# Linformer attention and a gated feed-forward in one kernel: all turns of batch 1 by DMA, later loads for batch 2, wider weight slices and one slice issued earlier

## Chip, cores and metric

One core of one Trainium2 chip runs the kernel. The metric is device time in microseconds, the median over runs.

## The reference, cut

```python
k_proj = einsum('ks,bhsd->bhkd', E, k); v_proj = einsum('ks,bhsd->bhkd', F, v)   # 8 batches, 8 heads, 1024 x 64
scores = q @ k_proj^T / 8                 # 64 projected keys
attn   = softmax(scores); x = attn @ v_proj               # then [8192, 512]
out    = (silu(x @ w_gate) * (x @ w_val)) @ w_out         # d_ff 1536; float32 out
```

## The kernel before

Batches are numbered from 0, so "the second batch" is batch 1. Attention is split into two halves (`ch`) a batch and four units a half. Half a batch is also one chunk of 512 tokens of the feed-forward part, which goes through 12 features of 128 columns: a gate product, a value product, and a third of an output product of the previous chunk. Attention of the next batch is laid into slots between those products: slot 2t follows the gate product of step t, slot 2t+1 the value and output ones.

q must be turned before the scores, and the normalised scores must be turned before the product with v. Both turns exist in two forms:

```python
BY_DMA = [(b, ch) for b in range(1, B) for ch in range(CH)][1:]     # all halves from (1, 1) on

def u_T(b, u, at="a", eng=nc.scalar):        # q, on TensorE: four transposes and a copy from PSUM
    ...
    for n in range(4):
        nc.tensor.transpose(out=ps[:, n, :], in_=src[...], identity=ident_bf[:])
    copy(eng, t[:], ps[:])

def u_TD(b, ch):                             # q, half a batch at once, by DMA from SyncE
    t = aw.tile([P, 2 * H, P], BF16, name="qTd", tag="qTd")
    nc.sync.dma_start_transpose(out=t[:], in_=qb[b, ch][:].rearrange("p h j d -> p (h j d)"))

def u_A(b, u, eng=nc.vector): ...            # normalised scores, on TensorE: four transposes and a copy
def u_AD(b, ch): ...                         # the same, half a batch at once, by DMA from SyncE
```

GpSimd issues every load of q, k, v and the weights (float32 in HBM, bf16 in SBUF), in program order and between its normalisations `u_N`. As built, each load also waits for the landing of the eighth load before it. In the start:

```python
u_N(0, 0)
load_w_gv(1, 2, (1,))
...                                      # (cut) u_N(0, 2), u_N(0, 1): GpSimd waits for scores here
load_w_gv(2, 4)                          # gate and value weights of features 2 and 3: 256 columns
...                                      # (cut)
load_w_gv(4, 6)
load_q(0, 1)
for f in (6, 8, 10):
    load_w_gv(f, f + 2)
load_wo(0); load_wo(1); load_k(1)
```

The softmax here doesn't subtract the row's maximum and nothing guards it: scores larger than these inputs give would overflow.

## Time and profile before

| | before |
|---|---|
| time, median of its runs beside the changed kernel | 573.17 us (573.05 to 573.64) |
| span of the profile | 571.7 us |
| TensorE matmuls | 2971, busy 99% of the span |
| DMA transposes | 13 of q, 13 of normalised scores |
| TensorE holes after the first feed-forward product that wait for weights | 0.60 us (feature 6, gate) and 0.28 us (feature 6, value) |

The page and the timeline lines of before stand in the prediction. A timeline line gives start, length, engine, source line, operation, out<-in, shapes and count, and in brackets the idle time before it and what ended it. Its start times matter more than the lengths: a 512-column matmul is shown as 0.38 us, but the next one starts 0.216 us after it. A hole is a start-to-start distance beyond that.

### The profile page before, as it was taken

To read this page: it belongs to the slowest core of one execution; us is meant where nothing else is said; L and a number is where in the kernel's file an instruction comes from. 1 tells how busy PE (TensorE), PEld (TensorE's weight loads), DVE (VectorE), ACT (ScalarE), POOL (GpSimd) and SP (SyncE) were. 2 spreads that over 40 slices of the span, in tenths; PEclk is the share of its full clock that TensorE was granted. 3 is DMA by queue.
4 is the path that set the end of the run, shared out by engine and by line. 5 is a ranking of instruction groups with operands and counts; after the bars stand their busy time and mean duration, and the time that the engine had idled before them with its cause. 6 is when DMAs were issued, how large, how long until landed. Compare 5 with 4: busy or idle time off the path is not lost.

```text
span 571.7 us, 7944 instructions
## 1 busy us (share of the span) xinstructions
PE 564.2 (99%) x2971; PEld 268.5 (47%) x2971; DVE 336.6 (59%) x581; ACT 238.3 (42%) x421; POOL 109.2 (19%) x122
## 2 busy tenths in 40 slices
PE   8999999999999999999999999999999999999997
PEld 4644444444444444444444444444444444444444
DVE  3677566666466654666556665567546674554540
ACT  3555434354435434444335434354342543443232
POOL 6834121134002500124001330023200220000000
PEclk9999999999999999999999999999999999999999
DMA  9999993549901697038940499204990124100012
GB/s 202 176 199 206 202 177 77 89 71 197 202 29 47 113 192 148 19 75 129 196 100 37 64 176 196 63 20 90 196 176 37 44 50 75 38 37 23 33 38 92
DMA packets 106983, 61.86 MB, mean 108 GB/s; under 512 B 60096, under 2 KB 98240, under 8 KB 106944
## 3 DMA queue, kind: packets, MB, share of 16 engines
q0 software_dynamic: 42800, 29.36, 35.7%
q1 hardware_dynamic: 63232, 30.42, 24.7%
q10 hardware_dynamic: 912, 1.57, 1.0%
q8 instruction: 23, 0.38, 0.3%
q14 instruction: 16, 0.13, 0.1%
HBM read 60.29 MB, written 16.78 MB: 135 GB/s over the span
## 4 chain that ended last, share of the span: by engine, by line
PE 92%; DMA 3%; DVE 2%; POOL 1%; ACT 1%; issue 0%; DVEq 0%; POOLq 0%
PE yps L362 29%; PE vps L324 27%; PE gps L324 27%; PE kvp L149 3%; PE sc L229 2%; PE pv L287 2%; DMA wv<-in_moe_w_val_dram 2%; DMA qb<-in_q_dram 1%; DVE zz L244 1%; POOL AA L260 0%; POOL wg L117 0%; PE qTp L195 0%; DVE hT L348 0%; ACT xT L137 0%; DVE s L343 0%
## 5 line engine op out<-in xcount | busy, mean ns | idle before, releaser
L343 DVE SCALAR_TENSOR_TENSOR s<-th,gps 128x512 f32<-128x512 f32 x192 | 130.5, 680 | 139.2 <-ACT th L336 138.8
L324 PE MATMUL gps<-xT,wg 128*128 128x512 bf16 (+1 forms) x776 | 197.8, 377 | 0.7 <-DMA wg<-in_moe_w_gate_dram 0.4
L324 PE MATMUL vps<-xT,wv 128*128 128x512 bf16 (+1 forms) x776 | 197.5, 377 | 0.1
L362 PE MATMUL yps<-wo,hT 128*128 128x512 bf16 (+1 forms) x780 | 194.5, 376 | 0.0
L336 ACT ACTIVATE th<-gps 128x512 f32<-128x512 f32 x192 | 114.6, 597 | 163.4 <-PE gps L324 161.9
L348 DVE TENSOR_TENSOR hT<-s,vps 128x512 bf16<-128x512 f32 x192 | 132.0, 687 | 22.1 <-PE vps L324 1.5
L362 PEld LDWEIGHTS <-hT 128*128 128x128 bf16 x780 | 76.2, 98 | 89.9
L260 POOL TENSOR_TENSOR AAd<-ee,rr 128x512 bf16<-128x512 f32 x52 | 54.1, 1040 | 319.5 <-issue 178.1
L324 PEld LDWEIGHTS <-wv 128*128 128x128 bf16 x776 | 73.8, 98 | 83.2 <-issue 3.3
L324 PEld LDWEIGHTS <-wg 128*128 128x128 bf16 x776 | 74.0, 98 | 81.9 <-DMA wg<-in_moe_w_gate_dram 0.9
L372 ACT ACTIVATE ysb<-yps 128x512 f32<-128x512 f32 (+1 forms) x65 | 38.4, 590 | 78.1 <-PE yps L362 78.1
L137 ACT CAST xT<-pv 128x512 bf16<-128x512 f32 x63 | 36.7, 584 | 51.2 <-PE pv L287 50.3
L244 DVE TENSOR_REDUCE zz<-ee 128x8 f32<-128x512 f32 x64 | 43.5, 679 | 19.4 <-ACT ee L233 19.4
L233 ACT ACTIVATE ee<-sc 128x512 f32<-128x512 f32 x64 | 37.9, 596 | 18.0 <-PE sc L229 17.9
L287 PE MATMUL pv<-AT,BDV 128*128 128x512 bf16 x60 | 22.6, 379 | 0.0
L229 PEld LDWEIGHTS <-qTd 128*128 128x128 bf16 x208 | 16.0, 98 | 12.3
L229 PE MATMUL sc<-BD,qTd 128*128 128x128 bf16 x208 | 20.1, 219 | 0.0
L137 DVE CAST BDV<-kvp 64x256 bf16<-64x256 f32 x14 | 6.0, 427 | 22.1 <-ACT ks L159 19.1
L260 POOL TENSOR_TENSOR AA<-ee,rr 128x512 bf16<-128x512 f32 x11 | 11.4, 1038 | 36.3 <-DVE rr L246 34.4
L246 DVE RECIPROCAL rr<-zz 128x8 f32<-128x8 f32 x64 | 13.0, 203 | 6.7 <-DVE zz L244 0.5
L149 PE MATMUL kvp<-vb,FT 128*64 128x512 bf16 (+2 forms) x80 | 15.7, 339 | 0.3 <-ACT BDV L137 0.3
L149 PE MATMUL kvp<-kb,ET 128*64 128x512 bf16 (+1 forms) x72 | 15.5, 358 | 0.3 <-DVE kb L137 0.2
(51 smaller groups left out, 146.4 us busy)
## 6 DMA issues: line engine op xcount, KB each, us to landing
out_dram<-ysb SPq DMA_DIRECT2D x63, 256.0 KB, 2.4
qb<-in_q_dram POOLq DMA_DIRECT2D x15, 512.0 KB, 16.9
kb<-in_k_dram POOLq DMA_DIRECT2D x7, 1024.0 KB, 11.3
vb<-in_v_dram POOLq DMA_DIRECT2D x7, 1024.0 KB, 14.0
wo<-in_moe_w_out_dram POOLq DMA_DIRECT2D x2, 768.0 KB, 15.3
wg<-in_moe_w_gate_dram POOLq DMA_DIRECT2D x5, 256.0 KB, 9.6
wv<-in_moe_w_val_dram POOLq DMA_DIRECT2D x5, 256.0 KB, 10.2
kraw<-in_k_dram ACTq DMA_DIRECT2D x2, 512.0 KB, 5.0
```

The costliest lines, as they stand in the source:

```text
L137: (nc.scalar.copy if eng is nc.scalar else eng.tensor_copy)(out=out, in_=in_)
L149: nc.tensor.matmul(out=t[lo : lo + 64, h0:h1].rearrange("p h d -> p (h d)"), lhsT=w[:, j, :], rhs=src[b][:, h0:h1, j, :], start=(j == 0), ...
L229: nc.tensor.matmul(out=ps[:, n, :], lhsT=t[:, n, :], rhs=BD[b % 2][:, 4 * g + n, :], start=True, stop=True)
L233: nc.scalar.activation(out=e[:].rearrange("p h j k -> p (h j k)"), in_=ps[:].rearrange("p a k -> p (a k)"), func=AF.Exp, scale=scale,)
L244: nc.vector.reduce_sum(out=z[:], in_=e[:], axis=AX.X)
L260: eng.tensor_tensor(out=a.rearrange("p j h k -> p h j k"), in0=ee.pop((b, u))[:], in1=rr.pop((b, u))[:].unsqueeze(3).to_broadcast([P, 4, 2 ...
L324: nc.tensor.matmul(out=ps[:, ts], lhsT=(wg, wv)[w][:, kt, f * P : (f + 1) * P], rhs=x[:, kt, ts], start=(kt == 0), stop=(kt == NKT - 1),)
L336: nc.scalar.activation(out=th[:], in_=ps[:], func=AF.Tanh, scale=0.5)
L343: nc.vector.scalar_tensor_tensor(out=s1[:], in0=th[:], scalar=1.0, in1=g[:], op0=ALU.add, op1=ALU.mult)
L348: nc.vector.tensor_tensor(out=hT[c][:, f, :], in0=s1[:], in1=ps[:], op=ALU.mult)
L362: nc.tensor.matmul(out=yy[c][:, cs], lhsT=hT[c][:, f, i * P : (i + 1) * P], rhs=wo[:, f, cs], start=(f == 0), stop=(f == NFT - 1),)
L372: nc.scalar.activation(out=ysb[:, cs], in_=yy[c][:, cs], func=AF.Copy, scale=0.5)
```

## The change

Its intent: take the last TensorE turns outside batch 0 off the busiest engine, place the loads so that the DMA turns come in time, and load weights in fewer and larger transfers. Core of the diff:

```diff
-BY_DMA = [(b, ch) for b in range(1, B) for ch in range(CH)][1:]
+BY_DMA = [(b, ch) for b in range(1, B) for ch in range(CH)]
 ...
         if b == 1:
+            put(22, u_TD, 1, 0)
+            put(29, u_KV, 1, "k")
+            put(32, u_KT, 1)
+            put(40, u_KV, 1, "v")
+            sa = (35, 36, 37, 38, 41, 42, 43, 44)
+            put(41, u_AD, 1, 0)
             put(30, u_TD, 1, 1)
-            (cut: k at 34, 36; u_T at 35 to 38; u_A at 41 to 44; second half's scores from 48)
+            put(47, u_AD, 1, 1)
 ...
-            if (b, j // 4) not in BY_DMA:
-                put(tt[j], u_T, b, j)
-                put(ta[j], u_A, b, j)
 ...
         load_w_gv(1, 2, (1,))
+        load_w_gv(2, 4)
 ...
-        load_w_gv(2, 4)
 ...
-        load_w_gv(4, 6)
+        load_w_gv(4, 8)
         load_q(0, 1)
-        for f in (6, 8, 10):
-            load_w_gv(f, f + 2)
+        load_w_gv(8, 12)
+        load_q(1, 0)
+        load_k(1)
         load_wo(0)
         load_wo(1)
-        load_k(1)
 ...
-        put(20, load_q, 1, 0)
 ...
-            s0 = 48 * (b - 1) - (12 if b == 2 else 24)
+            s0 = 48 * (b - 1) - (20 if b == 3 else 24)
+            at = (43, 43, 44, 45) if b == 2 else (s0, s0 + 2, s0 + 4, s0 + 6)
```

Batch 2's k and v projections move by eight slots to 56 and its two q transposes by six, to 57 and 59, since its loads now come later. Batch 3's loads move back by four slots.

More of the change, by code (lines that the diff above doesn't have):

```diff
@@ L394, in place @@
         if b == 1:
-            put(30, u_TD, 1, 1)
-            put(34, u_KV, 1, "k")
-            put(36, u_KT, 1)
-            put(40, u_KV, 1, "v")
-            sa = (37, 38, 39, 40, 48, 50, 52, 54)
-            tt = (35, 36, 37, 38)
-            ta = (41, 42, 43, 44)
-            put(57, u_AD, 1, 1)
-            sp = (43, 44, 45, 46, 66, 67, 68, 69)
-        else:
-            put(s0, u_KV, b)
-            put(s0 + 3, u_KT, b)
-            o = 14 if b == 2 else 6
-            put(s0 + (3 if b == 2 else -6), u_TD, b, 0)
-            put(s0 + (5 if b == 2 else -4), u_TD, b, 1)
+            put(22, u_TD, 1, 0)
[4 more added lines that the diff above has]
+            put(41, u_AD, 1, 0)
+            put(30, u_TD, 1, 1)
+            put(47, u_AD, 1, 1)
+            sp = (44, 45, 46, 46, 66, 67, 68, 69)
+        else:
+            put(s0 + (8 if b == 2 else 0), u_KV, b)
+            put(s0 + (11 if b == 2 else 3), u_KT, b)
+            o = 13 if b == 2 else 6
+            put(s0 + (9 if b == 2 else -6), u_TD, b, 0)
+            put(s0 + (11 if b == 2 else -4), u_TD, b, 1)
             sa = [s0 + o + 3 * j for j in range(NJ)]
@@ L555 @@
         for b in range(2, B):
-            s0 = 48 * (b - 1) - (12 if b == 2 else 24)
-            put(s0, load_k, b)
-            put(s0 + 2, load_v, b)
-            put(s0 + 4, load_q, b, 0)
-            put(s0 + 6, load_q, b, 1)
+            s0 = 48 * (b - 1) - (20 if b == 3 else 24)
+            at = (43, 43, 44, 45) if b == 2 else (s0, s0 + 2, s0 + 4, s0 + 6)
+            put(at[0], load_k, b)
+            put(at[1], load_v, b)
+            put(at[2], load_q, b, 0)
+            put(at[3], load_q, b, 1)
         for s in slots:
```

## The prediction

> **What bounds the kernel now.** I read the page's busy times first, then its slices, then the chain that ended last, and only then the timeline of the first 110 us.
>
> ```profile
> PE 564.2 (99%) x2971; PEld 268.5 (47%) x2971; DVE 336.6 (59%) x581; ACT 238.3 (42%) x421; POOL 109.2 (19%) x122
> PE   8999999999999999999999999999999999999997
> DMA  9999993549901697038940499204990124100012
> GB/s 202 176 199 206 202 177 77 89 71 197 202 29 47 113 192 148 19 75 129 196 100 37 64 176 196 63 20 90 196 176 37 44 50 75 38 37 23 33 38 92
> PE 92%; DMA 3%; DVE 2%; POOL 1%; ACT 1%; issue 0%; DVEq 0%; POOLq 0%
> ```
>
> TensorE holds 92% of the chain; no other engine is over 59% busy. A busy TensorE need not be a full one, so I checked spacing: in steady state groups of four 512-column matmuls follow one another every 0.86 us, without a hole. Adding the excess of each start-to-start distance over that spacing, I find nothing between 100 and 550 us beyond the fixed 0.1 us around the K and V projections. The kernel is thus a TensorE instruction stream plus a start of about 25 us and a few holes before 60 us. Only two things can move the time: TensorE instructions that go, and holes that close or open. The holes that the change touches are these, from the timeline and the list of waits:
>
> ```profile
> 31.27 1.03 PE L324 MATMUL vps<-xT,wv 128*128 128x512 bf16 x4
> 32.74 1.04 PE L324 MATMUL gps<-xT,wg 128*128 128x512 bf16 x4 [0.44 <-DMA wg<-in_moe_w_gate_dram]
> 33.61 0.39 PE L195 MATMUL qTp<-ident_bf,qb 128*128 128x128 bf16 x4
> 34.12 1.04 PE L324 MATMUL vps<-xT,wv 128*128 128x512 bf16 x4
> ```
> ```profile
> PEld L324 <- DMA wg<-in_moe_w_gate_dram: 0.9, 1, 0.9
> PEld L324 <- DMA wv<-in_moe_w_val_dram: 0.3, 1, 0.3
> ```
>
> The gate matmuls of feature 6 were due at 31.27 + 0.86 = 32.13 and started at 32.74: 0.6 us late. The value matmuls were due at 33.61 + 0.22 = 33.83 and started at 34.12: 0.3 us late. Together 0.9 us of waiting for weights of features 6 and 7. The holes at 24.9 us (0.26, a PSUM bank that VectorE frees), 43.7 (0.14) and 47.3 (0.46, copies of xT) have other causes and should stay.
>
> **What the Trainium skill says.** "TensorE: Matmul & The Clock Gate", section "Wait — 56ns, not 53.3ns?": warm matmuls start 55.6 ns apart at 128 columns and 215.7 ns at 512. The trace agrees: four 512-column ones take 0.86 us from group to group, and four 128-column ones 0.22 us (66.06 to 66.28 here). The 219 ns below is thus latency, not what a transpose costs.
>
> ```profile
> 66.06 0.39 PE L195 MATMUL qTp<-ident_bf,qb 128*128 128x128 bf16 x4
> 66.28 1.03 PE L324 MATMUL gps<-xT,wg 128*128 128x512 bf16 x4
> ```
> ```profile
> L195 PE MATMUL qTp<-ident_bf,qb x16: 219/219/230, 62.5 to 67.5; 128*128 128x128 bf16 x16
> ```
> ```profile
> L276 PE MATMUL aTp<-ident_bf,AA x16: 219/219/219, 75.2 to 80.5; 128*128 128x128 bf16 x16
> ```
>
> "DMA: Bandwidth & Descriptors", section "Issuing engines are not separate DMA queues": transfers started by any engine run on the same 16 DMA engines and interleave. The trace agrees: the transpose of the second half of q of batch 1 held SyncE 7.29 us and landed at 75.96, 13.0 us after its issue, while 2 MB of the third batch's k and v were in flight; one issued at 87.68 with nothing else in flight landed in 4.4 us.
>
> ```profile
> 63.00 7.29 SPq L207 DMA_TRANSPOSE qTd<-qb  x1
> 102.64 1.32 SPq L214 DMA_TRANSPOSE AT<-AAd  x1
> ```
>
> Same page, section "Why small descriptors are slow (HBM only)": each packet has a fixed overhead. The trace's packets agree in direction: a 512 B packet takes 60 ns, one of 1024 B 98 ns. In rate this is little here: 196 GB/s while 256-column weight slices stream, 204 while k and v do.
>
> **The change, part by part.** A slot is a place between matmul groups: slot 2t follows the gate matmuls of step t, slot 2t+1 the value and output ones.
>
> *Turns by DMA.* Gone from TensorE: 4 x 4 transposes of q and 4 x 4 of the normalised scores, 32 in all. In groups of four, 8 x 0.219 = **1.75 us**, all in the gapless stretch from 62 to 81 us, so all on the path. Off ScalarE go four copies of 0.585 us, off VectorE four of 0.41 us; neither bounds. Added are two DMA transposes, no engine time that counts. The build's order confirms 64 TensorE rows fewer (32 loads, 32 matmuls), and otherwise a reordering.
>
> *Where the new waits are.* Times below are those of before, shifted by what is removed. (a) The q transpose of half 0 waits for q(1,0), now loaded ahead of k(1): about 40 us by the sums below; landing by 53 even at 13 us, needed at slot 35, about 62.5. (b) Half 1: q(1,1) lands near 63 as before (62.98); with the third batch's loads held back behind the fifth normalised unit (not before 78), the transpose runs on quiet queues, 4.5 to 5.5 us, 68 to 69; needed at slot 41, about 73.7. (c) Scores back: the scores of unit 3 run at about 66.5. Before, such scores at 67.14 had their normalised tile at 70.50 + 1.04 = 71.54, 4.4 us on. So the tile is ready near 71, its transpose lands at the 4.3 us of the one issued at 102.64, near 75.5; the first matmul that needs it is in slot 44, about 78.9. **3.4 us of slack, the tightest place.** (d) Third batch: k, v, q issued from 78 to 82, 3 MB at 204 GB/s (15 us), with a 0.5 MB transpose between: k and v by 92, needed at slot 56 near 96; the q transpose by 103, needed at slot 61 near 105. All these hide, by 2 to 9 us. From the fourth batch on nothing differs.
>
> *Weights.* Two pieces. The slice of features 2 and 3 is issued before the two normalisations of batch 0 instead of after. GpSimd idles 1.89 us there until 17.28, and two issues of 0.8 us from 15.39 end by about 17.0 (the second needs the transfer four earlier, landed at 16.13): no delay, but 0.5 MB queued 3 us sooner. Before, the rate fell to 130 to 175 GB/s between 21 and 25 us against 196; about 0.16 MB was lost there, 0.85 us. So the value slice of features 2 and 3 lands at 24.4 instead of 25.3. Then slices of 512 columns: 0.5 MB at 204 GB/s is 2.57 us each. Gate of 4 to 7 at 27.0, value at 29.6, q(0,1) at 32.3, gate of 8 to 11 at 34.9. Needed: gate of 4 at 28.68, value of 4 at 29.55, q(0,1) near 33.0, gate of 8 near 37. So the 0.9 us at features 6 and 7 goes, and a wait of 0 to 0.7 us, say 0.3, may open at feature 4, whose value weights now arrive only with those of 7. Net **-0.6 us**. The output weights, behind q(1,0) and k(1), land near 51 and 55 with the first transpose beside them; needed at 55.5 and 60.
>
> Sum: 573.2 - 1.75 - 0.6 = **570.9 us**, 0.4% faster.
>
> **Rivals.** *1. The value weights of feature 4 eat the gain.* If the dip in rate is not cured (its second half, at 24 to 26 us, came although transfers were queued), value 4 to 7 lands at 30.4 and the wait is 0.9: about 571.4. For it: margin nil by my sum. Against: larger slices keep more bytes in flight. *2. A transposed tile comes late.* In-order TensorE stops for the scores' return in slot 44; at a landing like the 13 us of the contended case it would be 9 us late in place of 3.4 early: 577 to 580. For it: this batch is loaded and turned within 40 us, and ScalarE, VectorE and SyncE queues all stand in that path. Against: the loads that made that transpose slow are moved away by the same change. A milder form, 1 to 2 us, gives 572 to 573. *3. The transposes are hidden anyway,* so that removing them gives nothing. Against: TensorE has no gap there, and the copies they feed are not what it waits for. Would give 572.6. *4. Everything fits:* no new wait, 573.2 - 1.75 - 0.9 = 570.6.
>
> **Range and chances.** Below 570.3 I see no source: the other holes have other causes. The runs of before spread 0.6 us. Rivals 1 and 4 fill 570.3 to 571.6; the mild form of 2 reaches 572.4. Range 569.9 to 572.4. Two per cent is 11.5 us, more than all TensorE holes after the start together, so faster has 1%. Slower needs rival 2 at its full size in two places: 1%. Same 98%.
>
> **What would show it.** Right: TensorE matmuls 2971 - 32 = 2939; no wait for weights at features 6 and 7; at most one short one near 29.5; no wait of TensorE on the two transposed tiles; batch 1's second q transpose landing in about 5 us instead of 13. Wrong: a TensorE gap ahead of scores or value products between 60 and 82 us or at 95 to 106, or a wait for q(0,1) near 33 us over 0.5 us. The number fails if any one of these exceeds 1.5 us, or if holes that I called fixed (24.9, 43.7, 47.3) close.

## The result

571.45 us (571.23 to 571.71, four runs) against 573.17 us: the ratio is 0.9969, 95% interval 0.9951 to 0.9986, 0.3% faster. The page of the changed kernel, busy times, slices and chain:

```profile
PE 562.7 (99%) x2939; PEld 266.8 (47%) x2939; DVE 335.0 (59%) x577; ACT 236.8 (42%) x417; POOL 106.2 (19%) x118
PE   8999999999999999999999999999999999999997
DMA  9999879839903696039931399005990213010002
GB/s 208 198 204 196 153 122 201 142 60 203 201 18 75 109 180 138 37 56 159 188 79 38 74 176 212 37 20 104 189 187 20 56 39 75 37 38 37 20 37 94
PE 92%; DMA 4%; DVE 1%; POOL 1%; ACT 1%; issue 0%; DVEq 0%; POOLq 0%
```

The reader is to see 32 matmuls fewer, still a TensorE chain, and a different pattern of traffic in slices 5 to 9. The timeline of the changed kernel at features 4 to 6, where before waited at feature 6:

```profile
28.07 1.03 PE L324 MATMUL gps<-xT,wg 128*128 128x512 bf16 x4
29.60 1.04 PE L324 MATMUL vps<-xT,wv 128*128 128x512 bf16 x4 [0.51 <-DMA wv<-in_moe_w_val_dram]
...
31.34 1.03 PE L324 MATMUL vps<-xT,wv 128*128 128x512 bf16 x4
32.20 1.03 PE L324 MATMUL gps<-xT,wg 128*128 128x512 bf16 x4
33.06 0.39 PE L195 MATMUL qTp<-ident_bf,qb 128*128 128x128 bf16 x4
33.29 1.03 PE L324 MATMUL vps<-xT,wv 128*128 128x512 bf16 x4
```

The gate product of feature 6 (32.20) now starts exactly 0.86 us after the value product before it (31.34), and its value product 0.22 us after the q transposes (33.06 to 33.29): both old holes are gone. In their place the value product of feature 4 was due at 28.07 + 0.86 = 28.93 and started at 29.60, a new hole of 0.67 us. So 0.88 us of holes went and 0.67 came, **0.2 us net**.

Three transposes of batch 1 had to come in time: q of its first half (new), q of its second half, and the scores of its first half (new). They are shown from SyncE's timeline of the changed kernel (a length here is how long the issue held SyncE), followed by the first products that need the first and the last of them:

```profile
40.19 7.14 SPq L207 DMA_TRANSPOSE qTd<-qb  x1
63.93 1.73 SPq L207 DMA_TRANSPOSE qTd<-qb  x1
70.85 1.93 SPq L214 DMA_TRANSPOSE AT<-AAd  x1
```
```profile
61.97 0.39 PE L229 MATMUL sc<-BD,qTd 128*128 128x128 bf16 x4
78.66 0.38 PE L287 MATMUL pv<-AT,BDV 128*128 128x512 bf16 x1
```

Before, q of the second half held SyncE 7.29 us; now 1.73. By the trace's landing records it landed at 68.20, 4.3 us after issue, against 13.0 before. The scores' transpose landed at 75.09, 3.6 us before 78.66. The first one, beside the loads of k and of the output weights, landed at 58.16, 3.8 us before 61.97.

In sum, the profile's TensorE stream is 1.75 us of transposes and 0.2 us of holes shorter. The rest of the difference of the spans (571.7 to 569.4) is the start and the end. The first feed-forward product began at 21.24 us in before's profile and at 20.63 in this one. In all the profiles the start lies between 20.6 and 21.2 us (e3 and e4, which have the change's early issue, began at 21.06 and 20.96), so I count that as scatter.

The end is no scatter. The part after the last matmul's start was 3.3 us long before and 3.7 here, and every profile agrees: 3.30 to 3.31 us in the three with the old turns (before, e2, e9), 3.66 to 3.70 in the nine with the new ones. The last store lands 2.32 us after the last matmul's start in both; after it SyncE passes two semaphore waits of the program's closing sequence before, and eight, 0.06 us apart, in the changed kernel. Which part of the turns' edit orders these waits so was not tested. The new turns are thus worth 1.75 - 0.37 = 1.4 us, and the whole change 1.95 - 0.37 = 1.6 us, beside the 1.7 us of the timed runs.

### The profile page after: what moved, and what is told of

It reads as the page before. It is cut to its first block, busy times and chain, and to the rows that moved or that the text cites. A ratio compares the mean times of both kernels' runs of the same rounds, so it can differ in the third digit from the quotient of the medians.

```text
span 569.4 us, 7875 instructions
## 1 busy us (share of the span) xinstructions
PE 562.7 (99%) x2939; PEld 266.8 (47%) x2939; DVE 335.0 (59%) x577; ACT 236.8 (42%) x417; POOL 106.2 (19%) x118
## 4 chain that ended last, share of the span: by engine, by line
PE 92%; DMA 4%; DVE 1%; POOL 1%; ACT 1%; issue 0%; DVEq 0%; POOLq 0%
PE yps L362 29%; PE vps L324 28%; PE gps L324 28%; PE kvp L149 3%; PE sc L229 2%; PE pv L287 2%; DMA vb<-in_v_dram 2%; DMA wv<-in_moe_w_val_dram 2%; DVE zz L244 0%; DVE hT L348 0%; ACT xT L137 0%; POOL qb L107 0%; DVE s L343 0%; POOL AA L260 0%; PE kTp L174 0%
## 5 line engine op out<-in xcount | busy, mean ns | idle before, releaser
L260 POOL TENSOR_TENSOR AAd<-ee,rr 128x512 bf16<-128x512 f32 x56 | 58.2, 1041 | 343.3 <-issue 156.9
L229 PEld LDWEIGHTS <-qTd 128*128 128x128 bf16 x224 | 17.2, 98 | 13.2
L229 PE MATMUL sc<-BD,qTd 128*128 128x128 bf16 x224 | 21.6, 219 | 0.0
L107 POOL DMA_DIRECT2D qb<-in_q_dram x17 | 15.6, 920 | 0.0
```

The source lines that it names most:

```text
L229: nc.tensor.matmul(out=ps[:, n, :], lhsT=t[:, n, :], rhs=BD[b % 2][:, 4 * g + n, :], start=True, stop=True)
L260: eng.tensor_tensor(out=a.rearrange("p j h k -> p h j k"), in0=ee.pop((b, u))[:], in1=rr.pop((b, u))[:].unsqueeze(3).to_broadcast([P, 4, 2 ...
```

## Experiments

Ten kernels ran, all with correct results. They ran in three groups on different chips, and "before" was timed again beside each (573.1 to 573.2 us); across groups, compare by the ratios. From the first group on, most profiles lack 56 matmul records at even distances, so their matmul counts are not compared.

### e1_turns_only: the change without its weights' part

```diff
-        load_w_gv(1, 2, (1,)); load_w_gv(2, 4)      ... load_w_gv(4, 8); load_q(0, 1); load_w_gv(8, 12)
+        load_w_gv(1, 2, (1,))  ... (after two u_N) load_w_gv(2, 4)  ... load_w_gv(4, 6); load_q(0, 1); load_w_gv 6, 8, 10
```

> The changed kernel with its weights loaded as in the kernel before (256-column slices, the slice of features 2 and 3 after the two normalisations), all else of the change kept. Theory (the 32 transposes were on the path, 1.75 us; the weights' part brought only 0.2): 1.75 us under the kernel before, 571.4, with the two holes of before at features 6 and 7 back at 0.9 us together. Prediction on record (weights' part brings 0.6): also 1.75 under before, but 0.6 over the changed kernel. Rival (the turns are hidden anyway): within 0.3 us of the kernel before, and some other TensorE hole opens that eats the 1.75.

Measured: 571.75 us against 573.21, ratio 0.9973 (0.996 to 0.9985), 1.5 us. The timeline shows the old holes again (the due times are 31.11 + 0.86 = 31.97 and 33.33 + 0.22 = 33.55):

```profile
31.11 1.03 PE L324 MATMUL vps<-xT,wv 128*128 128x512 bf16 x4
32.46 1.04 PE L324 MATMUL gps<-xT,wg 128*128 128x512 bf16 x4 [0.32 <-DMA wg<-in_moe_w_gate_dram]
33.33 0.39 PE L195 MATMUL qTp<-ident_bf,qb 128*128 128x128 bf16 x4
33.83 1.04 PE L324 MATMUL vps<-xT,wv 128*128 128x512 bf16 x4
```

They are 0.76 us together. From 1.75 us, 0.1 us less of holes than before and 0.37 us more at the end, 1.5 us was to be expected. So the turns with their loads alone give about what the whole change gives, and the rival that turns are hidden anyway falls: 1.75 us lies inside the interval (0.9 to 2.3 us), 0.3 does not.

### e2_weights_only: the weights' part on the kernel before

```diff
         load_w_gv(1, 2, (1,))
+        load_w_gv(2, 4)             # early
 ...
+        load_w_gv(4, 8); load_q(0, 1); load_w_gv(8, 12)      # in place of slices of 256
```

> The kernel before with the weights' part of the change alone (512-column slices for features 4 to 11, the slice of 2 and 3 ahead of the two normalisations). Theory: the 0.9 us at features 6 and 7 goes and one wait of about 0.67 us opens at the value matmuls of feature 4, so 0.2 us under the kernel before, 573.0. Prediction on record: wait of 0.3, so 0.6 under, 572.6. Rival (the change owes its gain to the weights, turns being hidden): 1.7 under, 571.5.

Measured: 572.99 against 573.21, ratio 0.9995 (0.9982 to 1.0007). That excludes the rival (1.7 us), but does not tell 0.2 from 0.6. In its profile the wait at feature 4 was 0.15 us, with the first feed-forward product at 20.97 us; that profile is of the fastest of its five runs (572.42), so the wait of a median run is not shown.

### e3_small_first: features 4 to 7 in two slices

```diff
-        load_w_gv(4, 8)
+        load_w_gv(4, 6)
+        load_w_gv(6, 8)
```

> The changed kernel with features 4 to 7 in two 256-column slices again, in one stretch ahead of q(0,1); 8 to 11 stay in 512 columns. Theory (the wait at feature 4 is for the far half of a slice too large): value weights of 4 and 5 land near 27.2 us in place of 29.56, needed at about 28.9, so the wait of 0.67 us goes, nothing opens elsewhere, and the time falls by 0.6 to 0.7 against the changed kernel, about 570.8. Rival (the rate, not the slice, makes it late: smaller packets bring the dips back, and a wait moves to feature 6 or 7): within 0.2 us of the changed kernel, a hole of 0.3 or more at features 4 to 7.

Measured: 571.27, ratio 0.9965 (0.9953 to 0.9978). That is 0.2 us under the first four runs of the changed kernel and level with the five later ones (571.25, below), so no gain is shown, as the rival said of the time. Neither theory held as written: the wait at feature 4 went, as the first said, but another came, at neither place that the second named. It is at the value product of feature 8 (due at 37.61 + 0.22 = 37.83):

```profile
37.61 0.39 PE L229 MATMUL sc<-BD,qT 128*128 128x128 bf16 x4
38.28 1.04 PE L324 MATMUL vps<-xT,wv 128*128 128x512 bf16 x4 [0.28 <-DMA wv<-in_moe_w_val_dram]
```

The wide value slice of features 8 to 11 landed at 38.23 there; in the changed kernel it landed at 38.03 and was needed at 38.08. The wait at feature 4 had thus hidden a second one just like it.

### e7_all_small: all of features 4 to 11 in 256 columns, the early issue kept

```diff
-        load_w_gv(4, 8)
+        load_w_gv(4, 6)
+        load_w_gv(6, 8)
         load_q(0, 1)
-        load_w_gv(8, 12)
+        load_w_gv(8, 10)
+        load_w_gv(10, 12)
```

> The changed kernel with all of features 4 to 11 in 256-column slices, the slice of 2 and 3 still early, q(0,1) behind 4 to 7. Theory (a wait opens wherever a slice's far half is loaded ahead of need; the stream's total is not late): value weights of 4 and 5 land near 27.3 and those of 8 and 9 near 36.5 in place of 38.0, so neither the wait at feature 4 nor the 0.44 us that the run with small slices for 4 to 7 alone had at feature 8 is there; 0.4 to 0.7 under the changed kernel, 570.8 to 571.1. Rival (stream rate: 512-byte packets at 196 against 204 GB/s and more issues in flight make later tiles late): a hole appears at feature 6, 10 or 11 or at k of batch 1, and the time is within 0.2 us of the changed kernel.

The changed kernel itself ran beside it:

> The changed kernel itself once more, beside the next three on one chip. Theory: 1.7 to 2.0 us under the kernel before, 571.3 to 571.5, a wait of 0.1 to 0.7 us at the value matmuls of feature 4, larger where the first feed-forward matmul starts earlier, since the weights land at the same time (about 29.5) either way; no wait at the two transposed tiles of batch 1.

Measured: changed kernel again 571.25 us (571.21 to 571.29), ratio 0.9966 (0.9954 to 0.9979), wait at feature 4 of 0.63 us. With all slices small: **570.80 us** (570.66 to 571.21), ratio 0.9959 (0.9947 to 0.9972), the fastest by its median. Its timeline from feature 4 on, in steps of 0.86 us with no bracket:

```profile
28.14 1.03 PE L324 MATMUL gps<-xT,wg 128*128 128x512 bf16 x4
29.00 1.03 PE L324 MATMUL vps<-xT,wv 128*128 128x512 bf16 x4
29.86 1.03 PE L324 MATMUL gps<-xT,wg 128*128 128x512 bf16 x4
```

Value weights of 4 and 5 landed at 27.15, those of 8 and 9 at 35.16. No matmul of this profile waits for a gate or value weight. The next wait in the line is the q transposes of batch 0's second half, which started 0.08 us late at 32.53, when q(0,1) had landed at 32.48. The wide slices therefore cost the changed kernel about 0.45 us; the 4% higher rate that they bring (204 against 196 GB/s) does not pay for waiting for features 6 and 7 before 4 may start. The Trainium skill, "Perfetto Trace Analysis", section "DMA Optimizations", has both sides of this: larger transfers use the bandwidth better, and splitting may let some start sooner. Here the second decides, by 570.80 to 571.25 us, although the page's advice to split is for DMA engines that are generally idle, and here they were busy for 90% or more of the time from 14 to 43 us (digit 9 in e7's page).

### e8_copy_on_dve: one copy of xT moved to VectorE

```diff
-        put(23, u_PV, 0, 1, 3)
+        put(23, u_PV, 0, 1, 3, dve)      # on top of e7_all_small
```

> The same with the last of the four copies of xT of batch 0's second half on VectorE beside the third on ScalarE, in place of one behind the other. Theory (the holes of 0.19 and 0.27 us at 46.5 and 46.9 are the two copies in a row): the second of them goes, 0.25 us less, 570.6 to 570.8, the best of all. Rival (VectorE is itself behind there): the hole stays 0.4 or grows, no gain.

Measured: 570.91 us, ratio 0.996 (0.9948 to 0.9973): no gain, as the rival said. The copy waits behind VectorE's own work and takes longer. VectorE started its copy at 46.43, after two feed-forward operations in a row, and it lasted 0.68 us, so the last gate product started at 47.16:

```profile
45.82 0.69 DVE L348 TENSOR_TENSOR hT<-s,vps 128x512 bf16<-128x512 f32 x1
...
46.43 0.68 DVE L137 CAST xT<-pv 128x512 bf16<-128x512 f32 x1
...
47.16 0.38 PE L324 MATMUL gps<-xT,wg 128*128 128x512 bf16 x1 [0.26 <-DVE xT L137]
```

The hole in front of it was 0.42 us, against 0.27 with both copies on ScalarE. That is only a part of what this profile lost against e7's: its q transposes of batch 0's second half also started 0.38 us late in place of 0.08, because the feed-forward part began earlier (20.56 us against 20.69) and q(0,1) landed later (32.65 against 32.48). The edit does not touch that load.

### e5_slice_late: the slice of features 2 and 3 late again, wide slices kept

```diff
         load_w_gv(1, 2, (1,))
-        load_w_gv(2, 4)
 ...
+        load_w_gv(2, 4)             # after u_N(0, 2) and u_N(0, 1)
```

> The changed kernel with the slice of features 2 and 3 issued after the two normalisations as before, the 512-column slices kept. Prediction on record (0.85 us of the weights' part is the early issue): value weights of 4 to 7 land 0.6 to 0.85 us later than in the changed kernel, the wait at feature 4 grows by that, and the time to 572.1 to 572.3. Rival (the early issue brings only the 0.2 us that the landing of this slice showed against the start of that run): 571.6 to 571.7, wait at feature 4 larger by 0.2.

Measured: 572.25 us (571.86 to 573.07), ratio 0.9983 (0.9969 to 0.9996); 1.0 us over the changed kernel of the same rounds. The timeline has both weights of feature 4 late (due at 27.51 + 0.86 = 28.37, and 28.96 + 0.86 = 29.82):

```profile
27.51 1.03 PE L324 MATMUL vps<-xT,wv 128*128 128x512 bf16 x4
28.96 1.04 PE L324 MATMUL gps<-xT,wg 128*128 128x512 bf16 x4 [0.43 <-DMA wg<-in_moe_w_gate_dram]
31.47 1.04 PE L324 MATMUL vps<-xT,wv 128*128 128x512 bf16 x4 [1.47 <-DMA wv<-in_moe_w_val_dram]
```

That is 0.59 + 1.63 = 2.2 us in this profile, the slowest of its timed runs, with the value slice landing at 31.42 against 29.50. That landing is 1.9 us later, more than the 0.6 to 0.85 expected; the time was as expected. The prediction's 0.85 us for the early issue was near the 1.0 us of the medians; the rival's 0.2 us is too small.

### e9_early_issue_alone: only that slice early, on the kernel before

> The kernel before with one thing changed: the slice of features 2 and 3 issued ahead of the two normalisations. All slices stay at 256 columns, all turns as before. Theory (the early issue, not the slice width, is what the weights' part gains by): weights of 6 and 7 land 1.2 to 1.6 us earlier, the two holes of 0.9 us together go, none opens; 0.6 to 0.9 under the kernel before, 572.3 to 572.6. Rival (the wide slices are needed too): 0.3 us or less under before, with a hole left at features 6 or 7.

Its edit is the single line of e5, the other way round, on the kernel before. Measured: 572.47 us against 573.11 by the medians; one of the six runs took 574.35, as one of before's eleven took 574.80, so the ratio is 0.9994 (0.9978 to 1.0009) and the time alone settles nothing. The profile does: no matmul waited for a gate or value weight. The weights of 6 and 7 landed at 31.33 and 32.64, against 32.69 and 34.07 before, and the products of feature 6 start on time (30.96 + 0.86 = 31.82, 32.69 + 0.22 = 32.91):

```profile
30.96 1.03 PE L324 MATMUL vps<-xT,wv 128*128 128x512 bf16 x4
31.82 1.03 PE L324 MATMUL gps<-xT,wg 128*128 128x512 bf16 x4
32.69 0.39 PE L195 MATMUL qTp<-ident_bf,qb 128*128 128x128 bf16 x4
32.91 1.03 PE L324 MATMUL vps<-xT,wv 128*128 128x512 bf16 x4
```

So the early issue alone closes before's two holes, without any wide slice.

### e4_loads_early: batch 2's loads at their old slots

```diff
-            at = (43, 43, 44, 45) if b == 2 else ...
+            at = (36, 38, 40, 42) if b == 2 else ...
```

> The changed kernel with the third batch's loads not behind the fifth normalised unit of the second but early, in slots 36 to 42, as in the kernel before. Theory (holding them back is what lets all turns of batch 1 run by DMA): q's second transpose, issued near 64, again takes about 13 us and lands near 77, needed at 73.4, and the scores' transpose behind it lands near 85, needed at 78.7; TensorE stops for 3 us and then 3 to 5 more, 575 to 578. Rival (queues have room, transposes share at little cost): both land within 6 us of issue, no TensorE hole, 571.5.

Measured: 582.7 us, ratio 1.0169 (1.0154 to 1.0185), 11 us over the changed kernel. The rival falls. The theory holds in kind, but not in which transpose fails: that of q landed at 71.08, 7.1 us after issue and in time. That of the scores was issued at 71.09, beside the loads, held SyncE 7.77 us and landed at 88.25, 17.2 us on. SyncE and TensorE of this run:

```profile
71.09 7.77 SPq L214 DMA_TRANSPOSE AT<-AAd  x1
```
```profile
78.68 0.39 PE L229 MATMUL sc<-BD,qTd 128*128 128x128 bf16 x4
88.29 0.61 PE L287 MATMUL pv<-AT,BDV 128*128 128x512 bf16 x1 [9.22 <-DMA AT<-AAd]
```
```profile
core 0: us, PE busy (x) PEld busy (x) DVE busy (x) ACT busy (x) POOL busy (x), PEclk, DMA share, GB/s
79.00:88.00 9.00, 0.07 (x2) 0.00 (x0) 1.36 (x3) 0.97 (x2) 1.28 (x2) 0.61 1.44 160
88.00:92.00 4.00, 3.49 (x10) 1.43 (x12) 1.28 (x2) 0.59 (x1) 0.00 (x0) 0.59 0.47 88
```

TensorE was due at 78.90 and stood 9.4 us. The last fence, busy time by stretch, gives the granted clock in its third last column (the two after it are not used here): 0.61 in the stop and 0.59 in the 4 us after it. The matmuls there start 0.43 us apart in place of 0.216 and cost another 1.5 us, which makes up the 11. "TensorE: Matmul & The Clock Gate", section "Part 1: The HAM clock gate", says that an idle window of about 3.4 us puts the array back to half rate. This trace agrees on half rate (0.50 in every full microsecond from 82 to 91 us), but the clock fell sooner: it was 1.00 up to 81 us and 0.53 in the microsecond from there, so the fall came at about 81.1, some 2 us after the last matmul ended (79.07).

### e6_q_late: batch 1's first half of q loaded where it was before

```diff
-        load_q(1, 0)
-        load_k(1)
         load_wo(0)
         load_wo(1)
+        load_k(1)
 ...
+        put(20, load_q, 1, 0)
```

> The changed kernel with the first half of batch 1's q loaded where it was before, behind the output weights and k, from slot 20. Theory (the early load is what pays for the DMA turn of that half): it lands near 56, its transpose, beside v and the other half of q, takes over 10 us and lands near 68 to 72; needed at 62, so TensorE stops 6 to 10 us in front of the scores of batch 1, 577 to 582. Rival (there was slack, the order is cosmetic): no hole, 571.3.

Measured: 573.31 us, ratio 1.0004 (0.9991 to 1.0017), about 2 us over the changed kernel. That is the theory's kind at a third of its size or less: TensorE was due at 60.37 + 1.73 = 62.10 and stood 2.0 us, where 6 to 10 was expected. q landed at 52.85, and its transpose at 64.03 after 11.2 us, earlier than I had put both:

```profile
60.37 1.89 PE L362 MATMUL yps<-wo,hT 128*128 128x512 bf16 x8
64.08 0.40 PE L229 MATMUL sc<-BD,qTd 128*128 128x128 bf16 x4 [1.83 <-DMA qTd<-qb]
```

Without the early load of this half, its DMA turn gives back all that the change gains.

## Why the prediction was right

The time (571.45 in 569.9 to 572.4) was right, and the mechanism as well; the class, with 2% at 11.5 us, was hardly in doubt. The gain was over-estimated: 2.35 us by its sum, 1.7 measured. Two losses that it did not see, 0.4 us in the weights and 0.37 at the end, account for the difference within the scatter; they have the same sign, so no error hid another. By its own steps:

- **Turns by DMA, 1.75 us, all on the path: shown.** 32 matmuls went, no TensorE wait on batch 1's tiles came, and e1 kept 1.5 us of gain without any of the weights' part. What the sum missed is the 0.37 us longer end that came with the new turns.
- **Loads held back are what lets the second turns run: shown** by e4, where undoing that alone costs 11 us. Rival 2 was thus the right danger, and 577 to 580 undersized it, since the prediction did not count the cold clock after a stop.
- **Slack of the turns: right to hide, wrong as to the tightest.** The prediction named 3.4 us "the tightest place" though its own figures gave a q transpose of the third batch 2 us (103 for 105). The scores' transpose landed at 75.09 for 78.66, close to "75.5 for 78.9". But the first transpose of q took 18.0 us, not 13, and landed at 58.16 for 61.97; and the first q transpose of batch 2 landed at 104.60 for 105.11 (0.5 us). In the second profile of the changed kernel it landed at 105.12 and the scores waited about 0.1 us. That one, not the scores' return, is the tightest.
- **Weights, -0.6 us net: the mis-sized term.** The prediction said "a wait of 0 to 0.7 us, say 0.3, may open at feature 4"; it measured 0.67 and 0.63 us, so the net is 0.2. The landings were right (value slice of features 4 to 7: 29.6 predicted, 29.56; output weights: 51 and 55, 50.49 and 55.63). The time of need was not: I took 29.55 from a profile whose feed-forward part began at 21.24 us, and in the changed kernel's two profiles it began at 20.6. The landing moved little in the profiles with both edits (29.4 to 29.8). Where TensorE waits for a fixed landing, an earlier start only makes the wait longer.
- **The parts of that term.** The early issue at 0.85 us was near the 1.0 us of e5. The wide slices, which the prediction counted as gain, cost 0.45 us (e7). With the new turns all four combinations were run, and each edit has the same effect whichever way the other stands:

| medians, us | slice of 2 and 3 late | early |
|---|---|---|
| features 4 to 11 in 256 columns | 571.75 (e1) | 570.80 (e7) |
| in 512 columns | 572.25 (e5) | 571.25 (changed kernel again) |

(e1 ran in another group, beside a "before" that agrees within 0.1 us.)
- **Rival 3, hidden turns:** excluded by e1. **Rival 1** is the one that came, at 0.67 us of its 0.9; but the dip in rate was not its cause: from 20 to 25 us the core moved 157 GB/s before and 197 after.
- **Small misreadings.** The load that an issue waits for is the eighth before it, not "the transfer four earlier" (its landing at 16.13 is right). The transpose issued at 87.68 did not run "with nothing else in flight": a store of 256 KB, issued at 87.24, landed at 89.65. And the fourth batch (batch 3) does differ: its loads come four slots later.

What stays open: whether the 0.6 us by which the starts of two profiles differ has a cause in the change. Ten kernels' profiles scatter over the same range, and no run was made to test it. Open too is which edit lengthens the end by 0.37 us.

## What to carry to other kernels

When one engine has no gaps, an instruction taken off it is worth its start-to-start distance, not its listed length, provided that what replaces it comes in time; a DMA transpose should be placed where bulk loads are not in flight, and the loads moved if need be. In a start that is fed by a load stream, issue early and slice so that the first part needed is not tied to parts needed later: of two edits in the same lines one gained about 1 us and the other lost half of that. After closing one wait, look for the next behind it.

## What the Trainium skill lacked or had wrong

- "DMA: Bandwidth & Descriptors", section "Latency and other measured facts", gives an effective rate for a DMA transpose, but nothing on one that shares the engines: the same 0.5 MB transposes here landed 4.3 to 5.5 us after issue where no load was in flight and 6 to 18 us after issue beside loads, and held SyncE 1.3 to 7.8 us while being issued, with stores queued behind them.
- The same page, section "Measured (HBM→SBUF, 128 partitions, SWDGE, issued from GpSimd)", has 341 GB/s at 1 MB; loads that cast from float32 to bf16 wrote 196 GB/s (512 B packets) to 204 GB/s (1024 B) here. As each byte written stands for two read, that is 392 to 408 GB/s read, so the page's figure is not contradicted; but no page has a figure for loads that cast, nor says which side to count.
- "Perfetto Trace Analysis", section "DMA Optimizations", lists larger transfers first, and splitting for DMA engines that are generally idle; for a stream that TensorE follows closely, halving the slices won 0.45 us with the engines 90% busy or more and in spite of the lower rate.
- "TensorE: Matmul & The Clock Gate" holds in what was tried: 0.22 us for four 128-column matmuls, 0.86 for four of 512, and half rate in a 9.4 us stop. But the clock fell about 2 us after the last matmul, where the page gives an idle window of about 3.4 us.
